# A fused attention and gated-MLP kernel: the first operand loaded in three pieces, five products over zeros ahead of the first scores, and a new table of due times

## The chip, the cores and the metric

The kernel runs on one core of one Trainium2 chip. The metric is device microseconds from launch to end; the kernel before was timed in three runs, with a median of 621.24 us (621.21 to 621.81). Differences of some tenths of a per cent are therefore about as small as can be told from no change.

Engines are named as the profile names them: PE is TensorE's matrix product, PEld its weight load, DVE is VectorE, ACT is ScalarE, POOL is GpSimd, and SP (SPq) is SyncE, which issues all of this kernel's transfers. Each engine works its own instructions strictly in the order in which the program lists them, so an instruction that waits holds back all that stand behind it on the same engine.

## The reference

```python
# q, k, v: (4, 12, 448, 64) f32; w_gate, w_val: (768, 1536); w_out: (1536, 768)
scores = np.matmul(q, k.T) / sqrt(64)             # causal: masked above the diagonal
attn = exp(scores - max);  attn = attn / (attn.sum(-1) + 1e-09)
x = np.matmul(attn, v)                            # reshaped to (1792, 768)
gate = 1.0 / (1.0 + np.exp(-(x @ w_gate)))
out = (gate * (x @ w_val)) @ w_out
```

## The kernel before, in words

There are 4 batches of 12 heads. Two heads make a pair (64 + 64 partitions), so there are 24 pairs, six to a batch. Per pair, `load` (L268) brings q and k, transposed, into a tile `raw` of 896 columns, and a small extra piece for the last block into a tile `sm`; `load_v` (L282) brings v. `score` (L288) computes the scores of the causal blocks 0 to 3, which have 128, 256, 384 and 448 keys, by `products` (L370, matmuls on L387). `softmax` (L398) takes each block from its PSUM tile with one masked minimum per head on DVE (L410), an exponential on ACT (L417), sums and a reciprocal on DVE (L426, L428) and a scaling on POOL (L438). In the opening, pairs 0 to 5, PE turns the result around (`trans`, L302, matmuls L313) and multiplies by v (`pv`, L326). From pair 6 on the turning is done by DVE and a trip through DRAM: `shift` (L442) writes a tile `tb`, sends it out (`pd<-tb`, L461) and brings it back in four pieces (`pt<-pd`, L464), and `wpv` (L468, matmuls L481) multiplies it by v (`vr`).

The MLP comes in two plain units (batches 0 and 1: `unit_items`, L582, matmuls L594) and one for batches 2 and 3 together (`pair_items`, matmuls L807). `weight` (L548) brings each weight block in as 64-bit words of 768 columns (`room<-in_wp`, L559), ACT and DVE turn it to f32 (L563, L565, L567), SP writes the f32 copy back (`wdram<-wr`, L570) for later units, and ACT with DVE or POOL splits it in a high and a low half (L575, L577). Every product of the MLP is three matmuls (high by high, high by low, low by high), each 448 columns wide; a group of six products, k = 0 to 5, fills one PSUM tile. The items of an attention step and of the MLP are merged on PE: as pairs of a batch are finished, the unit of that batch can start.

No order is written out by hand. `Plan.op` (L110) takes each step with its engine, a cost, what it reads and writes, and a due time. `Plan.order` (L156) hands due times back from each step to those it needs, adds a correction to some of them from the table `NUDGE` (L48, by the number of the step; L160), and then plays the program on a model of the engines: whenever an engine is free it takes, of the steps that the model has ready, the one with the earliest due time. The order of that play is the order in which each engine's instructions are emitted. A nudge below zero brings a step forward among those that are ready, one above zero puts it back; the chip then keeps to that order whatever is really ready.

`consts` (L248) builds the mask and the unit matrix on POOL. In `load`, pair 0 comes in two pieces, the first 512 and the last 384 columns; `_lay` (L1046) lays its columns out so that the first piece holds what blocks 0 and 1 need. Blocks 0 and 1 of a pair are one PE step, and their scores share one PSUM tile per head.

Of the kernel before, what the change touches and what calls it, by code (L numbers as in the profile page):

```python
# [8 lines left out]
F32 = mybir.dt.float32  # L9
# [198 lines left out]
def kernel(  # L208
# [21 lines left out]
    ident = new("ident", [128, 128], F32)  # L230
    mask = new("mask", [128, ZM + WQ + HALF], F32)
# [16 lines left out]
    def consts():  # L248
# [7 lines left out]

        fill(mask, 0.0)
# [10 lines left out]
    def load(n):  # L268
        j = pairs[n]
        j["raw"] = r = new("raw", [128, 2 * S], F32, BUFS["raw"])  # L270
        cols = (0, 4 * WQ, 2 * S) if n == 0 else (0, 2 * S)
        for e, (a, c) in enumerate(zip(cols, cols[1:])):
            keys_ = (e,) if n == 0 else (0, 1)
            plan.op("SP", dma(128 * (c - a) * 4), lambda a=a, c=c: nc.sync.dma_start(
                out=r.t[:, a:c], in_=qkt[n][:, a:c]), writes=[(r, *keys_)], extra=2.8)
# [12 lines left out]
    def score(n, blocks, due):  # L288
# [9 lines left out]
        needs = [(j["raw"], *((0,) if blocks[-1] == 1 else (0, 1)))] + ([(j["sm"][1], "x")] if blocks[-1] == 3 else [])  # L298
        burst((qk_cost(blocks), lambda: products(j, blocks), needs, [(p,) for p in sp]), due)
# [70 lines left out]
    def products(j, blocks):  # L370
        r, x = j["raw"], j["sm"][1]
        first = r is pairs[0]["raw"]
        q0 = lambda i: WQ * i + (S if first and i > 1 else 0)
        k0 = 2 * WQ if first else S
# [14 lines left out]
    def wscore(n, due):  # L389
# [5 lines left out]
        burst((1.95, lambda: products(j, range(NB)), [(j["raw"], 0, 1), (j["sm"][1], "x")], [(p,) for p in a + b]), due)  # L395
        return lambda: softmax(j, range(NB))

    def softmax(j, blocks):  # L398
        mn, su, r_ = j["mn"], j["sum"], j["r"]
        for i in blocks:  # L400
# [4 lines left out]
            for z in range(2):  # L405
# [7 lines left out]
                ), [(sp[z],), (mask, "end") if last and z else (mask,)] + ([(mn, (1, i))] if last and z else []),  # L413
                    [(sm, (i, z) if last else i), (mn, (to, i))])
            for z in heads:
                sm = j["sm"][z]
                plan.op("ACT", act(ne, 0, 1) + 0.01, lambda z=z, sm=sm, i=i, ne=ne, off=off: nc.scalar.activation(  # L417
# [677 lines left out]
```

## Time and profile before

| what | us |
|---|---|
| median of the runs (three) | 621.24 |
| the profiled execution, its own time | 620.8 |
| its span, first to last instruction | 619.1 |
| PE busy in it | 606.9 (98% of the span) |
| DVE, ACT, POOL busy | 439.7, 335.6, 310.6 |
| share of PE in the chain that ended last | 89% |
| PE's first and last product start | 3.47 and 615.07 |

The profile is one execution. A busy PE is one that has a product under way, so a product that waits before it starts is idle time, while one that runs at half pace is busy. The span is 1.7 us shorter than the time of the same execution, and that is 0.4 us below the median. The granted TensorE clock is 1.00 in all stretches. The DMA share is that of the core's 16 DMA engines.

### The profile page before, as it was taken

Reading aid. Unit: us, or ns where it says so; the run is one execution under the profiler, and the core shown is the slowest. Engines: PE = TensorE matmul, PEld = TensorE weight load, DVE = VectorE, ACT = ScalarE, POOL = GpSimd, SP = SyncE. Lnnn points to the kernel's source line nnn. Section 1 sums busy time; section 2 is a strip of 40 time slices with the busy share of each in tenths; the row PEclk is TensorE's granted clock in tenths of the full one; section 3 lists DMA queues with packets and bytes.
Section 4 is the critical chain, followed back from the end, with each engine's and each line's share of the span. In section 5 each row is a group of like instructions: output and inputs, shape, how many; then the busy total and the mean of one; then the engine's idle time right before and its main releaser. Section 6 shows DMA issues by size and latency. Waiting matters only on the chain.

```text
span 619.1 us, 11867 instructions
## 1 busy us (share of the span) xinstructions
PE 606.9 (98%) x4182; PEld 531.5 (86%) x4182; DVE 439.7 (71%) x1048; ACT 335.6 (54%) x754; POOL 310.6 (50%) x350
## 2 busy tenths in 40 slices
PE   6999999999999999999999999999999999999997
PEld 3578888898888888888888899989999989999996
DVE  5897999889855546544648766577754688999752
ACT  6996765675634755555558644434333443657420
POOL 5650534614300676767676676658664666611200
PEclk9999999999999999999999999999999999999999
DMA  8688999998999999878786886855533213534321
GB/s 299 203 308 314 344 370 378 376 397 320 364 396 339 321 365 344 293 245 319 269 323 247 281 311 238 276 199 189 179 110 95 77 52 103 159 117 142 112 75 60
DMA packets 54348, 153.35 MB, mean 248 GB/s; under 512 B 6032, under 2 KB 12432, under 8 KB 51984
## 3 DMA queue, kind: packets, MB, share of 16 engines
q1 hardware_dynamic: 54288, 152.59, 69.6%
q8 instruction: 33, 0.54, 0.3%
q14 instruction: 27, 0.22, 0.1%
HBM read 109.31 MB, written 43.25 MB: 246 GB/s over the span
## 4 chain that ended last, share of the span: by engine, by line
PE 89%; DMA 4%; DVE 3%; ACT 2%; issue 1%; POOL 0%; SPq 0%; DVEq 0%; ACTq 0%; POOLq 0%
PE m L594 39%; PE m L807 19%; PE s L807 10%; PE t L807 7%; PE m L481 5%; PE s L387 4%; PE t L387 2%; DMA raw<-in_qkt_dram 2%; DMA pd<-tb 1%; DMA vr<-in_vt_dram 1%; PE t L313 1%; ACT sm L417 1%; DVE wr L567 1%; DVE sm L410 1%; POOL sm L438 0%
## 5 line engine op out<-in xcount | busy, mean ns | idle before, releaser
L761 POOL TENSOR_TENSOR wl<-room,wh 128x384 fp32r<-128x384 f32 x84 | 98.0, 1190 | 56.0 <-ACT wh L760 56.0
L438 POOL TENSOR_SCALAR sm<-sm,r 128x384 f32<-128x384 f32 (+3 forms) x165 | 94.1, 591 | 63.6 <-DVE r L428 50.2
L594 PE MATMUL m<-xh,wh 128*128 128x448 f32 x288 | 107.3, 372 | 0.0
L594 PE MATMUL m<-xh,wl 128*128 128x448 f32 x288 | 105.3, 366 | 0.0
L594 PE MATMUL m<-xl,wh 128*128 128x448 f32 x288 | 105.2, 365 | 0.0
L417 ACT ACTIVATE sm<-sm,mn 128x384 f32<-128x384 f32 (+3 forms) x168 | 87.6, 524 | 18.6 <-DVE mn L410 15.2
L577 POOL TENSOR_TENSOR wl<-wr,wh 128x768 fp32r<-128x768 f32 x38 | 70.6, 1872 | 24.1 <-ACT wh L575 20.8
L575 ACT CAST wh<-wr 128x768 fp32r<-128x768 f32 x72 | 59.8, 832 | 33.4 <-DVE wr L567 15.0
L760 ACT CAST wh<-room 128x384 fp32r<-128x384 f32 x84 | 39.8, 511 | 52.5 <-PE s L807 12.7
L410 DVE CUSTOM_DVE_ANT_0 sm<-s,mask 128x128 f32<-128x128 f32 (+3 forms) x108 | 42.5, 408 | 25.8 <-PE s L387 25.7
L594 PEld LDWEIGHTS m<-xh,wh 128*128 128x128 f32 x288 | 54.1, 188 | 6.6 <-issue 1.6
L594 PEld LDWEIGHTS m<-xh,wl 128*128 128x128 f32 x288 | 54.1, 188 | 4.5
L594 PEld LDWEIGHTS m<-xl,wh 128*128 128x128 f32 x288 | 54.1, 188 | 4.1
L594 PE MATMUL m<-gh,wh 128*128 128x448 f32 x144 | 53.3, 370 | 0.0
L594 PE MATMUL m<-gh,wl 128*128 128x448 f32 x144 | 52.6, 365 | 0.0
L594 PE MATMUL m<-gl,wh 128*128 128x448 f32 x144 | 52.6, 365 | 0.0
L624 POOL TENSOR_TENSOR gl<-gt,gh 128x448 fp32r<-128x448 f32 x24 | 28.9, 1208 | 37.4 <-ACT gh L623 27.3
L807 PE MATMUL m<-pt,wh 128*128 128x448 f32 x150 | 44.8, 367 | 0.2 <-DVE xl L676 0.2
L453 DVE STREAM_TRANSPOSE room<-sm 128x384 f32<-128x384 f32 (+2 forms) x84 | 35.4, 449 | 8.8 <-POOL sm L438 8.4
L387 PE MATMUL s<-raw 64*64 64x128 f32 (+3 forms) x432 | 35.7, 390 | 4.6 <-DMA raw<-in_qkt_dram 3.5
L481 PEld LDWEIGHTS m<-pt,vr 128*64 128x64 f32 x720 | 33.5, 137 | 7.8 <-issue 4.3
L577 DVE TENSOR_TENSOR wl<-wr,wh 128x768 fp32r<-128x768 f32 x34 | 33.5, 984 | 7.9 <-ACT wh L575 7.4
(177 smaller groups left out, 1373.7 us busy)
## 6 DMA issues: line engine op xcount, KB each, us to landing
room<-in_wp_dram SPq DMA_DIRECT2D x36, 768.0 KB, 7.4
pt<-pd SPq DMA_DIRECT2D x72, 256.0 KB, 5.6
wr<-wdram SPq DMA_DIRECT2D x45, 384.0 KB, 4.6
room<-wdram SPq DMA_DIRECT2D x45, 384.0 KB, 3.6
wdram<-wr SPq DMA_DIRECT2D x36, 384.0 KB, 7.6
pd<-room SPq DMA_DIRECT2D x12, 1024.0 KB, 4.7
raw<-in_qkt_dram SPq DMA_DIRECT2D x23, 448.0 KB, 5.9
vr<-in_vt_dram SPq DMA_DIRECT2D x24, 256.0 KB, 5.3
```

What stands on the lines that cost most here:

```text
L387: nc.tensor.matmul(out=sp[z].t[c:c + 64, o:o + ne], lhsT=q, rhs=k)
L410: plan.op("DVE", dve(n), lambda z=z, i=i, sp=sp, sm=sm, n=n, o=o, f=f, lo=lo, to=to, first=first: nc.vector.tensor_tensor_reduce(out=sm.t[ ...
L417: plan.op("ACT", act(ne, 0, 1) + 0.01, lambda z=z, sm=sm, i=i, ne=ne, off=off: nc.scalar.activation(out=sm.t[:, off:off + ne], in_=sm.t[:, ...
L438: plan.op("PL", 0.24 + w / 1200, lambda sm=sm, e=e, o=o, w=w, z=z: nc.gpsimd.tensor_scalar(out=sm.t[:, o:o + w], in0=sm.t[:, o:o + w], sca ...
L453: plan.op("DVE", dve(128 * c) + 0.03, lambda sm=sm, i=i, o=o, c=c, at=at: nc.vector.transpose(out=tv()[:, :, at:at + 32 * c].rearrange("p ...
L481: nc.tensor.matmul(out=vp.t[64 * z:64 * z + 64, i * WQ:i * WQ + rows(i)], lhsT=v.t[:, c, z], rhs=src, start=(c == 0), stop=(c == i))
L575: plan.op("ACT", act(768), lambda: nc.scalar.copy(hi_.t, t.t), [(t,)], [(hi_,)])
L577: plan.op(eng, cost, lambda: at.tensor_tensor(out=lo_.t, in0=t.t, in1=hi_.t.bitcast(F32), op=ALU.subtract), [(t,), (hi_,)], [(lo_,)], lock ...
L594: nc.tensor.matmul(out=ps.t[:, :S], lhsT=a.t[:, k, :], rhs=b.t if isinstance(b, Buf) else b(), start=(first and z == 0), stop=(last and z ...
L760: plan.op("ACT", act(w), lambda: nc.scalar.copy(f(hi_.t), x()), [(src, at)], [(hi_, e)])
L761: plan.op("PL", 0.97, lambda: nc.gpsimd.tensor_tensor(out=f(lo_.t), in0=x(), in1=f(hi_.t).bitcast(F32), op=ALU.subtract), [(src, at), (hi_ ...
L807: nc.tensor.matmul(out=ps.t[:, :S], lhsT=a.t[:, kw, :], rhs=b.at, start=bool(first and z == 0), stop=bool(last and z == 2), skip_group_che ...
```

## The change

It has five parts.

1. `consts` gets a tile `idle` of 128 by 128, set to zero on DVE, and a PE step that multiplies it by itself five times into a PSUM tile that nobody reads. The step has due time 0.
2. `load` brings pair 0 in three pieces instead of two: 256 columns (what block 0 needs), 448 (the other keys, and block 1's queries) and 192 (the queries of blocks 2 and 3). `_lay` and `products` follow the new layout. A score step now waits for as many pieces as its block needs.
3. For pair 0, block 0 becomes a PE step of its own, due 0.3 ahead of block 1. In the planner DVE's read of a block now needs that block alone (the keys `(p, i)`), also in `wscore`.
4. The planner's cost of an exponential rises by 0.08.
5. The table `NUDGE` is replaced. Because four steps are new, a step with number n from 10 on has number n + 4 after. Among the entries that go: the first two weight loads (252 and 260, -9.6), and three steps of the trip through DRAM of one pair (808 and 811, +3.4, its DVE transposes; 813, +3.3, its `pd<-tb`). Among those that come: the load of pair 1's `raw` (43, -3.2); the load of one late pair's v (911, -6.1, was -0.9); the last DVE transpose and the `pd<-tb` of that pair (920 and 921, -2.6); and +9.8 to +12.4 on the product k = 1 of 16 weight groups (273, 337, 351, 367, 425, 441, 455, 471, 547, 561, 577, 743, 759, 803, 865, 879).

```diff
+    10: -6.1, 43: -3.2, 105: 5.3, 113: 2.4, 199: 2, 223: 14.4, 229: -6.4, 232: -5.5, 273: 9.8, 308: 3.8,
+    312: -1.1, 337: 9.8, 351: 9.8, 367: 9.8, 399: 4.9, 401: -0.5, 407: -6.5, 410: 4.9, 425: 9.8, 441: 9.8,
+    455: 9.8, 471: 9.8, 547: 9.8, 561: 9.8, 577: 9.8, 743: 9.8, 759: 9.8, 803: 9.8, 840: -1.8, 865: 12.4,
+    879: 12.4, 882: 2.6, 895: 2.6, 911: -6.1, 920: -2.6, 921: -2.6, 932: 1.8, 939: 4.8, 950: -1.7, 988: 3.4,
...
+    idle = new("idle", [128, 128], F32)
...
+        plan.op("DVE", 0.1, lambda: nc.vector.memset(idle.t, 0.0), writes=[(idle,)])
+        ps = new("t", [128, 512], F32, 2, PSUM)
+        plan.op("PE", 2.6, lambda: [nc.tensor.matmul(out=ps.t[:, :128], lhsT=idle.t, rhs=idle.t, start=True, stop=True)
+                                    for _ in range(5)], [(idle,)], [(ps,)], 0.0)
...
-        cols = (0, 4 * WQ, 2 * S) if n == 0 else (0, 2 * S)
+        cols = (0, 2 * WQ, S + 2 * WQ, 2 * S) if n == 0 else (0, 2 * S)
...
-        needs = [(j["raw"], *((0,) if blocks[-1] == 1 else (0, 1)))] + ([(j["sm"][1], "x")] if blocks[-1] == 3 else [])
-        burst((qk_cost(blocks), lambda: products(j, blocks), needs, [(p,) for p in sp]), due)
+        needs = lambda i: [(j["raw"], *range(min(i + 1, 3)))] + ([(j["sm"][1], "x")] if i == 3 else [])
+        if n < 1 and len(blocks) > 1:
+            for i in blocks[:-1]:
+                plan.op("PE", qk_cost((i,)), lambda i=i: products(j, (i,)), needs(i), [(p, i) for p in sp], due - 0.3)
+        here = blocks[-1:] if n < 1 else blocks
+        burst((qk_cost(here), lambda: products(j, here), needs(here[-1]), [(p, *here) for p in sp]), due)
...
-                ), [(sp[z],), (mask, "end") if last and z else (mask,)] + ([(mn, (1, i))] if last and z else []),
+                ), [(sp[z], i), (mask, "end") if last and z else (mask,)] + ([(mn, (1, i))] if last and z else []),
...
-                plan.op("ACT", act(ne, 0, 1) + 0.01, lambda z=z, sm=sm, i=i, ne=ne, off=off: nc.scalar.activation(
+                plan.op("ACT", act(ne, 0, 1) + 0.09, lambda z=z, sm=sm, i=i, ne=ne, off=off: nc.scalar.activation(
...
-    qkt[0] = np.concatenate([x[:, :2 * WQ], x[:, S:], x[:, 2 * WQ:S]], axis=1)
+    qkt[0] = np.concatenate([x[:, :WQ], x[:, S:], x[:, WQ:S]], axis=1)
```

## Rows read from the trace of the kernel before

**Rows 1.** Windows, by stage: length, busy PE, PEld, DVE, ACT, POOL, PEclk, DMA, GB/s.
```profile
3.47:10.00 6.53, 5.59 (x64) 3.12 (x64) 4.33 (x26) 4.47 (x17) 0.80 (x2) 1.00 0.94 292
20.00:40.00 20.00, 18.94 (x231) 11.70 (x222) 17.84 (x74) 17.77 (x56) 14.95 (x23) 1.00 0.77 255
80.00:120.00 40.00, 40.00 (x304) 35.37 (x304) 36.58 (x89) 25.41 (x55) 18.41 (x25) 1.00 1.00 376
160.00:182.00 22.00, 20.21 (x160) 18.28 (x159) 14.18 (x25) 8.77 (x13) 3.13 (x7) 1.00 1.03 397
```
**Rows 2.** Timeline of PE, 3 to 8 us: start, length, operation, count, idle before.
```profile
3.47 1.56 PE L387 MATMUL s<-raw 64*64 64x128 f32 x16 [3.47 <-DMA raw<-in_qkt_dram]
4.80 1.50 PE L387 MATMUL m<-raw 64*64 64x384 f32 x8
...
7.31 0.88 PE L387 MATMUL m<-raw 64*64 64x384 f32 x8 [0.46 <-DMA raw<-in_qkt_dram]
```
**Rows 3.** Timeline of PE around 28 us: the same first step of a later pair.
```profile
27.72 0.88 PE L387 MATMUL s<-raw 64*64 64x128 f32 x16
```
**Rows 4.** The chain that ended last, 40 to 60 us: start, length, what.
```profile
44.37 0.87 PE t L313 x8
```
**Rows 5.** Memset of a tile as large as the new one, on POOL, by tile.
```profile
L250 POOL MEMSET ident<- x1: 204/204/204, 1.3 to 1.3; 128x128 f32 x1
```
**Rows 6.** Timeline of SP's queue in the opening.
```profile
0.80 0.86 SPq L274 DMA_DIRECT2D raw<-in_qkt_dram  x2
...
2.18 0.43 SPq L274 DMA_DIRECT2D raw<-in_qkt_dram  x1
...
6.87 3.74 SPq L274 DMA_DIRECT2D raw<-in_qkt_dram  x2
```
**Rows 7.** Window of the first transfers, columns as in the first group.
```profile
1.75:3.42 1.67, 0.00 (x0) 0.00 (x0) 0.00 (x0) 0.33 (x1) 1.32 (x6) 1.00 0.92 288
```
**Rows 8.** Issue to landing, by tile: the first two pieces of pair 0.
```profile
DMA to landing us min/median/max: 2.6/2.6/2.6
```
**Rows 9.** Issue to landing: the small extra piece issued at 1.72 (`sm`).
```profile
DMA to landing us min/median/max: 4.2/4.2/4.2
```
**Rows 10.** Issue to landing: pair 1's load, issued at 2.18 (`raw`).
```profile
DMA to landing us min/median/max: 5.1/5.1/5.1
```
**Rows 11.** Timeline of DVE in the opening.
```profile
5.20 0.29 DVE L410 CUSTOM_DVE_ANT_0 sm<-s,mask 128x128 f32<-128x128 f32 x1 [5.20 <-PE s L387]
...
5.62 0.42 DVE L410 CUSTOM_DVE_ANT_0 sm<-s,mask 128x256 f32<-128x256 f32 x1
...
8.93 0.25 DVE L410 CUSTOM_DVE_ANT_0 sm<-s,mask 128x128 f32<-128x128 f32 x1
```
**Rows 12.** Timeline of PE, 160.9 to 162.7 and 178.9 to 180 us.
```profile
162.59 0.33 PE L481 MATMUL m<-pt,vr 128*64 128x128 f32 x2 [1.23 <-DMA vr<-in_vt_dram]
...
179.94 0.33 PE L481 MATMUL m<-pt,vr 128*64 128x128 f32 x2 [0.56 <-DMA vr<-in_vt_dram]
```
**Rows 13.** Timeline of SP's queue, 144 to 174 us.
```profile
144.42 0.33 SPq L559 DMA_DIRECT2D room<-in_wp_dram  x1
144.80 0.43 SPq L570 DMA_DIRECT2D wdram<-wr  x1
145.34 0.36 SPq L461 DMA_DIRECT2D pd<-tb  x1
...
153.05 2.55 SPq L464 DMA_DIRECT2D pt<-pd  x4
155.64 0.47 SPq L285 DMA_DIRECT2D vr<-in_vt_dram  x1
...
173.41 0.44 SPq L285 DMA_DIRECT2D vr<-in_vt_dram  x1
```
**Rows 14.** Issue to landing: the last two `pt<-pd` pieces issued near 172 us.
```profile
DMA to landing us min/median/max: 7.0/7.1/7.2
```
**Rows 15.** Timeline of PE, 20 to 22 us.
```profile
21.06 0.87 PE L387 MATMUL s<-raw 64*64 64x128 f32 x14 [0.62 <-DVE mn L410]
```

More of the change, by code (lines that the diff above doesn't have):

```diff
@@ L270, in load @@
         j["raw"] = r = new("raw", [128, 2 * S], F32, BUFS["raw"])
-        cols = (0, 4 * WQ, 2 * S) if n == 0 else (0, 2 * S)
+        cols = (0, 2 * WQ, S + 2 * WQ, 2 * S) if n == 0 else (0, 2 * S)
         for e, (a, c) in enumerate(zip(cols, cols[1:])):
-            keys_ = (e,) if n == 0 else (0, 1)
+            keys_ = (e,) if n == 0 else (0, 1, 2)
             plan.op("SP", dma(128 * (c - a) * 4), lambda a=a, c=c: nc.sync.dma_start(
@@ L372, in products @@
         first = r is pairs[0]["raw"]
-        q0 = lambda i: WQ * i + (S if first and i > 1 else 0)
-        k0 = 2 * WQ if first else S
+        q0 = lambda i: WQ * i + (S if first and i else 0)
+        k0 = WQ if first else S
         for i in blocks:
@@ L394, in wscore @@
         j["sp"] = {0: (a, 384), 1: (b, 0), 2: (a, 0), 3: (b, 256)}
-        burst((1.95, lambda: products(j, range(NB)), [(j["raw"], 0, 1), (j["sm"][1], "x")], [(p,) for p in a + b]), due)
+        burst((1.95, lambda: products(j, range(NB)), [(j["raw"], 0, 1, 2), (j["sm"][1], "x")], [(p, 0, 2) for p in a] + [(p, 1, 3) for p in b]), due)
         return lambda: softmax(j, range(NB))
```

12 rows, old and new, of the table NUDGE are left out of this document.

## The prediction

> **What bounds the kernel now.** I read the windows by stage first, then the chain that ended last, then the timelines of PE, DVE and SP in the two places where PE stands. In the windows the reader is to see that PE is busy for all 40 us of a middle stretch, and that the idle time of PE lies in three places: ahead of its first product at 3.47 and in the opening behind it (5.59 busy of 6.53, and 18.94 of 20.00 later), and 1.79 us in the 22 us from 160 on [rows 1, 2]. Whatever starts the full stretch earlier, or fills those 1.79 us, moves the end by as much; the products themselves are the same before and after. The second thing to see is that in the first third PE is not far ahead of its helpers: DVE is at 36.58 of 40 us and the DMA engines at a share of 1.00 there [rows 1]. So the end of that stage hangs on PE and on the transfers at once, and a lead that PE gains in the opening can be waited off at 160.
>
> **Working against which time.** The sum is made on the profiled execution: span 619.1, its own time 620.8, so 1.7 around it. The median of the runs, 621.24, is 0.4 above that; I take the sum off the median.
>
> **The opening.** Now: PE starts when the first piece has landed, at 3.47, and its 16 first products take 1.56 us, where the same step of a later pair takes 0.88; the next eight take 1.50 against 0.88 for the same shape at 7.31 [rows 2, 3]. These are half-pace against full-pace durations (1.2 and 2.4 GHz), though the granted clock is told as 1.00 throughout: what PE did before was nothing at all. Together they cost 0.68 + 0.62 = 1.30 us. DVE, which must take every block out of PSUM, starts at 5.20 because blocks 0 and 1 are one step [rows 11].
>
> The dummy products: a memset of this size took 0.20 us on POOL [rows 5]; DVE is free from 0.8 on (SP's first issue is at 0.80 [rows 6]), so PE can begin at about 1.1. Eight 128-column f32 records took 0.87 us at full pace [rows 4]; five products are ten records, 1.1 us at full pace and 2.2 at half. I take 2.2, since nothing ran before: they end at about 3.3 (bounds 2.2 and 3.3 by the row; by the planner's own cost of 2.6, at 3.7). The first piece has half the bytes: 131 KB less at 288 GB/s is 0.46 us off a landing at 0.80 + 2.6 = 3.4, so about 2.95 [rows 6 to 8]. The data no longer decide, the dummies do: block 0 starts at 3.3 instead of 3.47, at half pace takes 0.5 (a third of 1.56), and with the 0.17 from the last product to DVE's first read [rows 2, 11] DVE starts at about 4.0: 1.2 us earlier. The second piece, 229 KB, ends 98 KB later than the first piece of before, 0.34 us, so at 3.8, in time for block 1.
>
> What is late next: pair 1's load lands at 2.18 + 5.1 = 7.3, and PE waited 0.46 us for it [rows 2, 6, 10]. The third piece costs SP one more issue, 0.43 us (0.86 for two [rows 6]); but step 43 at -3.2 puts pair 1's load ahead of pair 0's small extra piece (by the planner's rule for due times the two stood at 2.8 and 0.3), so it is again the fourth issue, at 2.18. Step 10 at -6.1 is the second piece; the planner lets no write go before the first one of a tile, so nothing moves. It can land up to 0.5 us earlier (147 KB, 0.5 us at 288 GB/s [rows 7]), and the small piece, now landing at 1.72 + 4.2 = 5.9 [rows 9], falls to about 7.3. So DVE will have done blocks 0 to 2 of pair 0 by about 6.2 and then stand for about 1 us. It had all of pair 0 behind it at 8.93 [rows 11]; then it will have block 3 left, about 1.3 us with its sums, at 7.3, and be there at 8.3 to 8.6. **The lead that gets through is 0.3 to 0.6; bounds 0 (pair 1's load decides alone) and 1.2 (the whole of DVE's start). I take 0.6.**
>
> The first two weight loads lose their -9.6 and fall behind the loads of later pairs, among them the one issued at 6.87 [rows 6]. The bytes are the same, and the products that need them come late in the opening, whose transposes PE still works on at 44.37 [rows 4]; I cost this at nothing, covered by the opening's attention work of some 20 us, and at up to 1 us if that cover went. The 0.08 in the cost of an exponential and the keys in the planner change no instruction.
>
> **The stage at 160 to 182.** PE stands 1.23 us before the product at 162.59 and 0.56 us at 179.94, both times until v has landed; that is the whole 1.79 of the window [rows 1, 12]. First stand: `pd<-tb` is issued at 145.34, right behind a weight load (786 KB) and a write-back (393 KB) at 144.42 and 144.80; its return starts at 153.05 and v is issued behind it at 155.64 [rows 13]. The +3.3 that held this `pd<-tb` back, and the +3.4 on its transposes, are gone, so it should go ahead of those 1.18 MB, which at 397 GB/s are 3.0 us of transfer [rows 1]. The last transposes end just before 145.34, so the issue itself moves little; the landing can move by up to 3.0. That more than covers 1.23. Behind SP's wait for the transposes then stand the weight load and the write-back, delayed about 1 us; their readers are ACT and DVE in the queue for a later group. Second stand: v's load is brought forward by 5.2 more than before, ahead of the four return pieces; then the last return piece, which landed at about 172.0 + 7.2 = 179.2 [rows 14], is late next, 0.7 before 179.94: worth about 0.5. **Together 1.7 at most. I take 1.4; bounds are 0 (the wait only moves to the next transfer) and 1.79.**
>
> **The held products.** Sixteen products k = 1 are due 9.8 to 12.4 later, which is about twelve products of 0.6 us, so attention steps between them may go up to 7 us earlier on PE. PE has no idle time there to win, 40.00 of 40.00 [rows 1]. The gain is that scores reach DVE sooner, the cost that PE may stand at a step whose data are not there. Nothing in the trace shows the new order; bounds: -1.06, the idle time of 20 to 40 us [rows 1] filled, and +1.23 for one stand like that at 162.59 [rows 12]. I take 0, midway, because both rows are near.
>
> **Sum:** -0.6 - 1.4 + 0 = -2.0 us, span 617.1, median **619.2**.
>
> **A rule that speaks against the split.** The nearest row for a product that waits for a DVE read of scores is at 21.06: 0.62 us [rows 15]. Blocks 0 and 1 share one PSUM tile per head, so when DVE reads block 0 as block 1 is to be written, block 1 may have to wait until both heads are read: 5.20 to 5.62 and a short tail, about 0.5 us [rows 11]. Then DVE stands while block 1 runs, and blocks 0 to 2 end 0.5 to 0.7 later, at 6.9, still ahead of 7.3: the lead drops by 0.3, to a median of 619.5. The Trainium skill's page "PSUM — Partial Sum Buffer", section "PSUM bank collisions raise a hardware error", says that two engines must not be in one bank and partition quadrant at the same time, whatever columns they touch, and that software has to guard it; by that rule block 1 would wait. No row of the kernel before shows a write beside a read in one tile, so this is open.
>
> **The rivals.**
> *Bank wait*, as just priced: 619.5.
> *Absorbed.* The transfers, at a share of 1.00, keep their times, and PE only arrives earlier and waits longer. For it: DMA at 1.00 and 1.03 in the two stretches [rows 1], and both stands end with a transfer. Against it: the DMA share is 0.77 at 20 to 40 us, so the transfers too can start earlier. It gives 621.24 less nothing to 0.4: 621.0.
> *Warm-up does nothing.* PE runs the dummies at half pace, stands, and the scores still come at half pace or later (3.7 by the planner's cost): the lead is -0.2 to 0, the rest stays: about 620.0, just on the line.
> *Slower: the held products.* An attention step reaches PE before its last transfer or its DVE read is done, and PE, in order, stands there with ready MLP products behind it. There are six such steps, those of pairs 6 to 11. It decides against the change when two of them stand 1.3 us each beside the two stands that stay, which grow by the lead: +2.6 - 0.6 = +2.0, 623.2. For it: the planner's due times run ahead of the chip (the load issued at 155.64 stood in it under a due time of 143.6), so what its model has ready need not be ready. Against it: the same planner, equally off, gives 40.00 of 40.00 before.
>
> **How the numbers follow.** Forecast (619.2) 0.37, bank wait (619.5) 0.13, warm-up nothing (620.0) 0.10, half on each side, absorbed (621.0) 0.25, slower (623.2) 0.15. A measurement of this kernel tells 0.2%, 1.2 us, from no change: faster means below 620.0, slower above 622.5. Faster 0.55, same 0.30, slower 0.15. The range leaves out the slower rival and the far end of the gains: from 621.24 - 1.2 - 1.79 - 0.9 = 617.4 (both places at their bounds and most of the 1.06) to 621.9 (absorbed, with half a stand of 1.23 more).
>
> **What would show it.** Opening: PE's first product at about 1.1, block 0 at about 3.3, the 64x384 products at nearer 0.88 than 1.50, DVE's first read near 4.0; if pair 1's products still start at 7.3 the lead is what the steps say. Bank wait: block 1 starts only as DVE's second read ends. Stage: idle time of PE between 150 and 185 well below 1.79, `pd<-tb` ahead of the weight load, v not the last releaser. Held products: PE idle in the windows from 40 to 160 us, now 0. I am wrong if the wait for v only moves to the return pieces, or if PE's idle time appears at new attention steps.

## The result: slower by 0.9%, and the profile after

The changed kernel takes **627.6 us** (median of four runs, 627.01 to 628.37) against 621.52 for the kernel before: a ratio of 1.0089, with an interval of 1.0068 to 1.0111. The prediction was 619.2, range 617.4 to 621.9. The span of the profiled execution is 626.3 against 619.1: 7.2 us to account for.

To find where they lie I summed the columns of all matmul records in order of time (weighted by what a column of their shape takes at full pace, the products over zeros left out) and read how much later the changed kernel reaches each sum. This **lag** behind the profiled execution of the kernel before is used for all kernels below.

| time in the kernel before, us | 5 | 10 | 20 | 30 | 50 | 160 | 165 | 170 | 180 | 220 | 230 | 360 | 390 | 615 |
|---|---|---|---|---|---|---|---|---|---|---|---|---|---|---|
| lag of the changed kernel, us | 0.91 | 1.65 | 0.71 | -0.18 | 1.32 | 1.32 | -0.14 | 1.30 | 0.72 | 0.65 | 5.86 | 5.88 | 7.09 | 7.06 |

So 5.2 of the 7.1 us come at one place, between 220 and 230, and 1.2 more at 380. The opening and the stage at 160 to 182, on which the whole sum of the prediction stood, come out at a loss of 0.7 together: 1.3 lost by 50 us, and 0.6 won back between 160 and 180. From 50 to 160, where the held products lie, nothing changes.

**The opening.** Timeline of TensorE in the changed kernel (start, length, operation, count, idle before and its releaser); it answers to [rows 2]. Lines of the changed file lie 11 higher from the products on.

```profile
1.12 2.50 PE L262 MATMUL t<-idle 128*128 128x128 f32 x10 [1.12 <-DVE idle L260]
3.55 0.71 PE L398 MATMUL s<-raw 64*64 64x128 f32 x8
4.78 1.33 PE L398 MATMUL s<-raw 64*64 64x256 f32 x8 [0.52 <-DVE mn L421]
5.69 1.71 PE L398 MATMUL m<-raw 64*64 64x384 f32 x8
...
7.71 1.89 PE L398 MATMUL m<-raw 64*64 64x384 f32 x8
```

The five products run from 1.12 at half pace and end at 3.62, and block 0 follows at 3.55, no earlier than in [rows 2]; what comes sooner is its end, 4.26, since block 1 is no longer part of the step. Then TensorE waits 0.52 us, and not for data: the releaser is VectorE, which has to have read block 0 from the tile that block 1 goes into. The 64x384 products take 1.71 and 1.89, where [rows 2] has 1.50 and then 0.88: half pace lasts longer. VectorE, to be read against [rows 11]:

```profile
4.42 0.29 DVE L421 CUSTOM_DVE_ANT_0 sm<-s,mask 128x128 f32<-128x128 f32 x1 [3.36 <-PE s L398]
...
6.15 0.42 DVE L421 CUSTOM_DVE_ANT_0 sm<-s,mask 128x256 f32<-128x256 f32 x1 [1.22 <-PE s L398]
...
10.54 0.29 DVE L421 CUSTOM_DVE_ANT_0 sm<-s,mask 128x128 f32<-128x128 f32 x1 [0.78 <-PE s L398]
```

It reads block 0 at 4.42 instead of 5.20, block 1 at 6.15 instead of 5.62, and is at pair 1 at 10.54 instead of 8.93. The trace's record of the granted clock starts with the first stretch at full: at 9.97 us here, at 6.37 in the kernel before. Ahead of it the views print 1.00 for want of a record, which is why the windows show no change there; the durations do. So "1.00 in all stretches", as it stands ahead of the prediction, does not hold for the first 6.37 us of the kernel before.

**The two large places.** Windows of the changed kernel (columns as in [rows 1]), then its timeline of TensorE:

```profile
80.00:120.00 40.00, 39.85 (x302) 34.91 (x301) 36.90 (x91) 27.42 (x59) 16.03 (x21) 1.00 0.99 363
160.00:182.00 22.00, 20.94 (x150) 18.59 (x150) 15.52 (x22) 9.42 (x14) 2.33 (x4) 1.00 1.01 379
224.00:234.00 10.00, 6.24 (x72) 5.30 (x64) 3.09 (x17) 2.31 (x8) 3.34 (x4) 0.83 0.96 337
```

```profile
169.97 0.48 PE L605 MATMUL m<-gh,wl 128*128 128x448 f32 x1 [1.06 <-DVE wl L588]
...
229.04 3.34 PE L492 MATMUL m<-pt,vr 128*64 128x128 f32 x40 [3.76 <-DMA pt<-pd]
232.31 0.47 PE L605 MATMUL m<-xh,wh 128*128 128x448 f32 x1
...
381.08 2.00 PE L492 MATMUL m<-pt,vr 128*64 128x128 f32 x40 [0.91 <-ACT wh L771]
```

In the first window TensorE is busy for 39.85 of 40 us: the held products bring no stand. In the second it is 20.94 busy where [rows 1] has 20.21: the stands for v at 162.59 and 179.94 [rows 12] are gone as predicted, but one of 1.06 for a weight split has come at 168.9. At 225 TensorE stands 3.76 us for the probabilities of a pair to come back from DRAM (`pt<-pd`); the granted clock falls to half in that stand (0.83 over the window), and the 40 matmuls behind it take 3.34 us, where the same group of a later pair, at 381, takes 2.00. 3.76 + 1.34 = 5.1, the step of the table. SyncE's queue and GpSimd say why the return is late; SyncE in the changed kernel, then in the kernel before, then GpSimd in the changed kernel:

```profile
212.36 0.38 SPq L472 DMA_DIRECT2D pd<-room  x1
213.53 2.14 SPq L583 DMA_DIRECT2D wr<-wdram  x2
215.72 0.65 SPq L745 DMA_DIRECT2D wd<-wdram  x1
220.08 0.32 SPq L472 DMA_DIRECT2D pd<-room  x1
220.50 3.88 SPq L475 DMA_DIRECT2D pt<-pd  x4
```

```profile
210.06 0.33 SPq L461 DMA_DIRECT2D pd<-room  x1
...
215.90 1.80 SPq L464 DMA_DIRECT2D pt<-pd  x4
217.80 0.38 SPq L274 DMA_DIRECT2D raw<-in_qkt_dram  x1
220.97 0.32 SPq L461 DMA_DIRECT2D pd<-room  x1
```

```profile
206.50 2.67 POOL L449 TENSOR_SCALAR sm<-sm,r 128x384 f32<-128x384 f32 x5 [0.71 <-DVE r L439]
209.14 1.84 POOL L588 TENSOR_TENSOR wl<-wr,wh 128x768 fp32r<-128x768 f32 x1
210.95 0.73 POOL L449 TENSOR_SCALAR sm<-sm,r 128x128 f32<-128x128 f32 x2
```

A pair's probabilities go out at 212.36 and have landed at 219.26, but its four returns stand behind the *next* pair's send, which waits for VectorE's transposes until 220.08. So they go out from 220.50 and the last lands at 228.84; in the kernel before they went out from 215.90 to 217.27, ahead of that send, and had landed at 222.68, 1.7 us before TensorE came to them at 224.42.

So the last landing is 6.2 us later, for two reasons. The send itself is late: two of the pair's seven scalings now stand behind a weight split on GpSimd, so the send leaves 2.30 us later (212.36 for 210.06) and takes 6.90 us to land instead of 5.33, together 3.9. The rest, 2.3, is the order on SyncE: the returns start 1.24 us behind that landing instead of 0.51, and take 8.34 us from the first issue to the last landing instead of 6.78. The two don't simply add up in the stand. An estimate from these numbers: with the late send but the returns ahead of the next send, the last would land at 219.26 + 0.51 + 6.78 = 226.55, and TensorE, which is there at 225.28, would stand 1.3 us instead of 3.76. With the send in time but the returns behind the next send, they would still go out at 220.50, and the stand would be the same. So by this estimate the order carries most of the stand; no run changes it here without the send.

### The profile page after: what moved, and what is told of

Read it like the earlier page. It is cut to its first block, busy times and chain, and to the rows that moved or that the text cites. A ratio compares the mean times of both kernels' runs of the same rounds, so it can differ in the third digit from the quotient of the medians.

```text
span 626.3 us, 11881 instructions
## 1 busy us (share of the span) xinstructions
PE 613.2 (98%) x4192; PEld 536.6 (86%) x4192; DVE 446.1 (71%) x1049; ACT 334.9 (53%) x754; POOL 310.7 (50%) x350
## 4 chain that ended last, share of the span: by engine, by line
PE 84%; DVE 5%; DMA 5%; ACT 2%; POOL 1%; issue 1%; SPq 1%; DVEq 0%; ACTq 0%; POOLq 0%
PE m L605 35%; PE m L818 19%; PE s L818 10%; PE t L818 7%; PE m L492 5%; PE s L398 3%; DMA room<-in_wp_dram 3%; DMA pt<-pd 2%; PE t L398 2%; DVE sm L421 1%; POOL sm L449 1%; PE t L324 1%; DVE wl L588 1%; SPq L475 1%; DVE wr L578 1%
## 5 line engine op out<-in xcount | busy, mean ns | idle before, releaser
L449 POOL TENSOR_SCALAR sm<-sm,r 128x384 f32<-128x384 f32 (+3 forms) x165 | 91.8, 577 | 79.1 <-DVE r L439 57.5
L772 POOL TENSOR_TENSOR wl<-room,wh 128x384 fp32r<-128x384 f32 x84 | 96.4, 1168 | 60.4 <-ACT wh L771 56.4
L428 ACT ACTIVATE sm<-sm,mn 128x128 f32<-128x128 f32 (+3 forms) x168 | 87.7, 525 | 15.7 <-DVE mn L421 15.3
L492 PEld LDWEIGHTS m<-pt,vr 128*64 128x64 f32 x720 | 34.9, 141 | 10.8 <-issue 8.6
L492 PE MATMUL m<-pt,vr 128*64 128x128 f32 (+1 forms) x720 | 37.3, 260 | 4.8 <-DMA pt<-pd 3.8
L574 ACT ACTIVATE wd<-room 128x768 f32<-128x768 f32 x36 | 32.6, 911 | 17.1 <-DMA room<-in_wp_dram 17.1
```

The source lines that it names most:

```text
L428: plan.op("ACT", act(ne, 0, 1) + 0.09, lambda z=z, sm=sm, i=i, ne=ne, off=off: nc.scalar.activation(out=sm.t[:, off:off + ne], in_=sm.t[:, ...
L449: plan.op("PL", 0.24 + w / 1200, lambda sm=sm, e=e, o=o, w=w, z=z: nc.gpsimd.tensor_scalar(out=sm.t[:, o:o + w], in0=sm.t[:, o:o + w], sca ...
L492: nc.tensor.matmul(out=vp.t[64 * z:64 * z + 64, i * WQ:i * WQ + rows(i)], lhsT=v.t[:, c, z], rhs=src, start=(c == 0), stop=(c == i))
L574: plan.op("ACT", act(n) + 0.1, lambda: nc.scalar.activation(out=d.t.bitcast(F32), in_=hi().bitcast(F32), func=ACTF.Prelu, scale=REBIAS, al ...
L772: plan.op("PL", 0.97, lambda: nc.gpsimd.tensor_tensor(out=f(lo_.t), in0=x(), in1=f(hi_.t).bitcast(F32), op=ALU.subtract), [(src, at), (hi_ ...
```

## The experiments

All times are medians, and each ratio is to the kernel before, run beside it on the same chip; it need not be the quotient of two medians. Runs of one kernel spread over 1.6 to 6.3 us there (the kernel before: 620.3 to 626.7 in 141 runs), so ratios below 1.002 are hardly told from 1. Part of this spread has a name: in 32 of the 141 runs the mean granted clock is 0.997 or less, and they take 623.3 us at the median, the others 621.3. A profile is one execution and can be of either kind: those of f3, g3, h2 and h6 have a stretch at half clock, and for f3, g3 and h2 they lie 1 to 3 us above the median of their kernel. "Without N" and "with N" speak of entries of the table `NUDGE`, by the numbers of the changed kernel unless it is said otherwise (its steps are numbered four higher from the opening on).

**1. Which part costs the 6 us?** Four runs on the changed kernel and the one before.

```diff
 e1 (changed kernel)  -    1074: 2.9, 1075: 2.9, 1076: 2.9, 1077: 2.9,
 e2 (changed kernel)  its code; NUDGE = the table before, numbers + 4
 e3 (kernel before)   its code; NUDGE = the new table, numbers - 4
 e4 (changed kernel)  -  lambda: [nc.tensor.matmul(...) for _ in range(5)]   +  lambda: None
```

> The changed kernel without the four entries 1074 to 1077 (+2.9), which put the POOL scalings of one pair back. PE's order stays the same; in SP's queue the four return pieces of that pair come ahead of the next pair's send again. Theory A (the loss is one stand of PE at 225 us, set off by these entries): the stand of 3.8 us and the half-pace product group behind it (3.3 instead of 2.0) go, about -5 us, 622.4. Rival B (the loss is the opening, and the stand only shows a lead being waited off): the wait moves to a later product, 627 or more.

> The changed kernel's code (three pieces, five products, block 0 a step of its own) with the due-time table of the kernel before, every number plus 4. It tells the price of the code alone. Theory A: the code costs what the opening loses, 0.6 to 1.6 us, so 622.1 to 623.1, and there is no stand at 225. Rival B (the code carries most of the loss): 626 or more. My prediction's steps would have given 620.9.

> The kernel before with the new due-time table alone, every number minus 4 (entry 10 left out). Theory A: the stand at 225 us and its half-pace group come all the same, about +5 and +1 for the wait at 380: 626.5 to 627.5. Rival B: 621.5.

> The changed kernel with the five products over zeros not issued; order of everything else the same, so the output is unchanged. Theory: in the opening PE goes over to full pace at 9.97 us instead of 6.37 because block 1 waits for DVE, not because of the products; without them block 0 starts at 3.1 instead of 3.55 and the rest of the opening is within 0.5 us of the changed kernel, 627.1 to 627.6. Rival 1 (the products do warm PE): full pace comes later still, pair 1 takes longer, 628 to 629. Rival 2 (the products themselves put the change of pace off): full pace near 6.4, opening 1 to 1.5 us shorter, 626.3.

| run | us | ratio (interval) |
|---|---|---|
| e1 without four scalings' entries | 622.38 | 1.0009 (0.9991 to 1.0026) |
| e2 new code, old due times | 622.72 | 1.0026 (1.0011 to 1.0041) |
| e3 old code, new due times | 630.69 | 1.0145 (1.0120 to 1.0171) |
| e4 changed, no products | 627.12 | 1.0082 (1.0059 to 1.0106) |

Most of the cost lies in the table: e2 and e3 part code from table (the code alone costs 0.1 to 0.4%), and e1 shows that without four of its entries the stand at 225 is gone (lag 0.14 at 220, 0.24 at 230; the end 1.4). Those four are what puts the two scalings behind the weight split: the last one ends at 211.68 in the changed kernel and at 209.35 in e1, where the send leaves at 209.96 and the returns at 216.43, ahead of the next send. e3 came out 3 us above its expectation: with the old code the new table stands at 228.8 too (2.33), and besides loses 4.5 us between 15 and 40 us, whose cause I did not follow up. Leaving the products out (e4; nothing reads what they compute) changes nothing that can be measured.

**2. Is it those four entries, or the order that they make on SyncE?**

```diff
 g4 (kernel before)  +    1070: 2.9, 1071: 2.9, 1072: 2.9, 1073: 2.9,
 h1 (kernel before)  +    917: -2.6, 1073: 2.9, 1106: 6.8, 1123: 8.2, 1157: 0.6,
 h4 (kernel before)  +    917: -2.6,            1106: 6.8, 1123: 8.2, 1157: 0.6,
```

> The kernel before with 2.9 us added to the due times of four of its steps (1070 to 1073, the scalings that 1074 to 1077 are in the changed kernel; 1072 loses its own 0.5) and nothing else; the order of TensorE is unchanged, on GpSimd two of seven scalings fall behind a weight split, and on SP the four transfers that bring the probabilities back (pt<-pd) fall behind the next pair's room load. Theory A (these four entries alone are the cost): a stand of 2 to 4 us for pt<-pd between 220 and 230, with the 40 matmuls behind it at half pace if it is long: 625 to 627. Rival B (they cost only together with the rest of the new table): no stand there, 621.5.

> The kernel before with five entries of the new table (917, 1073, 1106, 1123 and 1157 here; 921, 1077, 1110, 1127 and 1161 in the changed kernel) added to its own: the smallest set found by which the planner again puts the four transfers that bring a pair's probabilities back (pt<-pd) behind the next pair's send (pd<-room) on SP. On TensorE one step changes place by three. Theory A (that order on SP is the cost of the changed kernel): a stand of 2.5 to 4 us for pt<-pd at 225, followed by 40 matmuls at half pace where the clock falls: 624 to 627. Rival B (the order alone costs little; it takes the late transposes or the rest of the table as well): 621.5 to 622.5.

> The same without the entry 1073, that is with four of the five: TensorE's order is the one of the run with five, but SP issues the four pt<-pd before the next pair's send, as in the kernel before. Theory A: no stand at 225, 621.5 to 622.2. Rival (the other four entries are the cost): 624 or more, as with five.

g4: 622.19 (1.0006, 0.9989 to 1.0024), no stand at 225. Its send is 1.3 us late too (211.40), but against its expectation the returns stay ahead of the next send (216.30 and 220.75). So the four entries do nothing alone; my theory fell in that form. In the planner's play the return falls behind the next send only when several small moves add up: played with one entry of the changed kernel's table left out at a time, it has the old order again for any one of 932, 988, 1074, 1077, 1087 and 1110. h1 is the smallest such set that I found for the kernel before, h4 the same without one of its five; both have the same order on TensorE. **h1: 628.40 (1.0105, 1.0081 to 1.0128), somewhat above its expectation. h4: 621.85 (1.0010, 0.9996 to 1.0025).** SyncE's queue and TensorE's timeline, h1 first, then h4:

```profile
212.94 0.38 SPq L455 DMA_DIRECT2D pd<-room  x1
...
220.94 0.32 SPq L455 DMA_DIRECT2D pd<-room  x1
221.36 3.37 SPq L458 DMA_DIRECT2D pt<-pd  x4
```

```profile
229.17 3.68 PE L475 MATMUL m<-pt,vr 128*64 128x128 f32 x40 [3.56 <-DMA pt<-pd]
232.78 0.74 PE L588 MATMUL m<-xh,wh 128*128 128x448 f32 x1
```

```profile
209.98 0.33 SPq L455 DMA_DIRECT2D pd<-room  x1
...
215.69 1.80 SPq L458 DMA_DIRECT2D pt<-pd  x4
219.82 0.32 SPq L455 DMA_DIRECT2D pd<-room  x1
```

```profile
224.34 2.00 PE L475 MATMUL m<-pt,vr 128*64 128x128 f32 x40
```

In h1 the returns are behind the next send, TensorE stands 3.56 us and goes on at half pace (3.68; 0.74 for the product behind it, where 0.37 is usual); in h4 they are ahead of it and the same group starts without a wait at 224.34. The lag of h1 goes from 0.97 at 220 to 7.11 at 230, that of h4 is about 0 at both. One due time tells the two kernels apart, and nothing else of the change is needed for the whole loss. That due time does two things, as in the changed kernel: it puts a scaling behind a weight split on GpSimd, so that the send leaves 3.0 us later (212.94 for 209.98), and it turns the order on SyncE. By the same estimate as above the late send alone would leave 1.7 of the 3.56 us.

**3. What does the opening give?** Block 0 gets tiles of its own (f1, f2, f4, g1), with and without the products; the products alone (g3); ones in place of zeros (g1).

```diff
 f1 (e1)             +        if n < 1 and len(blocks) > 1:
                     +            j["sp"][0] = ([new("t", [128, 512], F32, 2, PSUM) for z in range(2)], 0)
 f2 (f1)             as e4
 g3 (kernel before)  + the memset of `idle` and the five products, as in the change
 f4 (e2)             f1's edit; without 812, 815, 817; 911: -6.1
 g1 (f4)             - memset(idle.t, 0.0)   + memset(idle.t, 1.0)
```

> The changed kernel without entries 1074 to 1077 (as in the run with four scalings undone, 622.4), and block 0 of the first pair gets two PSUM tiles of its own, so that block 1's products need not wait until VectorE has read block 0. Theory A (the 0.5 us pause between block 0 and block 1 is what keeps TensorE at half pace until 9.4): products and scores run without a break from 1.1 us, the full clock is granted by 6.4 us at the latest, VectorE reads block 1 at about 5.2 instead of 6.16, TensorE stands ahead of the kernel before at 10 us by some 0.5 instead of 1.46 behind. Rival B (something else keeps the pace down): the full clock still comes after 8.5 us and the first reads of pair 1 at 10.3 or later. On the time: if an early lead is carried on, 621.4; if it is used up before 30 us, as the lag of 1.46 at 10 us was there, 622.4 as without the edit.

> The same without the five products over zeros (the step issues nothing; they compute nothing that is used). Theory A (an unbroken run of TensorE work brings the full clock): scores start at 2.9, the full clock comes about 2.9 us later, as in the kernel before (3.47 and 6.37), so near 5.9, some 1 to 2 us later than with the products; the time is within 0.4 us of the run with products. Rival (products are what brings the full clock): without them it comes after 8.5 us, as in the run without products and with shared tiles (9.4).

> The kernel before with the five products over zeros and their memset ahead of the first scores and nothing else of the change (its own due times; a handful of steps behind 250 us change places because the play starts otherwise). Theory A (the products don't bring the full clock forward, it follows the scores): full clock 2.9 to 4.5 us after the first scores, between 6.4 and 8, as in the three profiled runs of this code so far (6.37, 7.65, 7.92), time 621.5. Rival B (the change's aim): the scores that start at 3.5 run at full pace from 5 us at the latest, the first reads of pair 1 come 0.4 us or more earlier than 8.93, time 621.0.

> The kernel with own tiles and old due times (621.4, full clock from 6.65), with ones in place of zeros in the tile that the five products read. Rival A (products over zeros don't count as work for the clock): with ones the full clock comes before 5.5. Rival B (what the numbers are makes no difference): between 6.4 and 8. The time is the same, 621.4, in both, since an earlier clock meets the landing of pair 1's raw at 8.1.

| run | full clock from, us | first read of pair 1, us | lag at 10 us | us | ratio (interval) |
|---|---|---|---|---|---|
| before | 6.37 | 8.93 | 0 | | |
| g3 before, products | 7.18 | 9.11 | 0.12 | 621.71 | 1.0010 (0.9989 to 1.0030) |
| e1 shared tile, products | 9.39 | 10.36 | 1.46 | 622.38 | 1.0009 (0.9991 to 1.0026) |
| f1 own tiles, products | 7.52 | 9.50 | 0.88 | 622.05 | 1.0006 (0.9991 to 1.0021) |
| f2 own tiles, no products | 9.02 | 10.11 | 1.21 | 623.13 | 1.0008 (0.9988 to 1.0029) |
| f4 own tiles, old order | 6.65 | 9.71 | 0.75 | 621.37 | 0.9990 (0.9975 to 1.0005) |
| g1 the same, ones | 4.70 | 9.72 | 0.77 | 622.34 | 1.0006 (0.9993 to 1.0020) |

Own tiles take the pause away: TensorE in f1, and then in g1.

```profile
3.55 0.83 PE L392 MATMUL t<-raw 64*64 64x128 f32 x8
4.03 1.20 PE L392 MATMUL s<-raw 64*64 64x256 f32 x8
4.89 1.62 PE L392 MATMUL m<-raw 64*64 64x384 f32 x8
```

```profile
4.81 0.86 PE L392 MATMUL m<-raw 64*64 64x384 f32 x8
5.46 0.69 PE L392 MATMUL s<-raw 64*64 64x224 f32 x4
5.96 0.60 PE L392 MATMUL s<-sm 64*64 64x224 f32 x4
8.15 0.88 PE L392 MATMUL m<-raw 64*64 64x384 f32 x8 [1.59 <-DMA raw<-in_qkt_dram]
```

Three things follow. The bank wait is real and goes with the shared tile. When the full clock comes varies from execution to execution: the old opening without products, seven profiled executions of as many kernels, has it from 6.37 to 9.23; unbroken with products, eight, 4.70 to 7.52 (the early ones at 5.33 and 5.37 are with zeros, so ones are not what makes the 4.70); with products and the pause, three, 8.58 to 9.97; pause and no products, two, 9.02 and 9.41. So the products bring it forward by 0.8 us at the median (7.65 to 6.82), and the pause goes with the late end (f2, with tiles of its own, pauses too, 0.50 us until the second piece has landed); but the groups overlap, and one execution of each kernel doesn't settle more. And little of it gets through: in g1 the last two blocks of pair 0 ran at full pace, and then TensorE stands 1.59 us until pair 1's operand has landed at 8.10. That is the old order of the loads, in f4 and g1. With the new one pair 1's operand lands earlier, at 6.46 to 7.12, and TensorE waits for pair 0's own small piece instead, which lands at 7.20 to 7.46 in g2, h5 and f1; in g2:

```profile
7.24 0.41 PE L392 MATMUL s<-sm 64*64 64x224 f32 x2 [0.88 <-DMA sm<-in_qkt_dram]
```

In no run does the new opening reach pair 1's first read before 9.16 us, however early its clock, against 8.93 to 9.29 in five of the seven with the old one. My expectation that f1 would be ahead at 10 us was wrong. That the products are worth nothing is not shown with tiles of their own: f2, without them, takes 623.13 where f1 takes 622.05, and the intervals of their ratios overlap.

**4. Where does the gain at 160 go, and can both be had?**

```diff
 f3 (kernel before)  without 808, 811, 813; 907: -6.1            (its own numbers)
 h6 (kernel before)  new entries for 796 to 995 in place of its own
 g2 (f1)             the old table from step 1300 on
 h2 (f1)             the old table from step 300 on
 h3 (h2)             and the new one from 800 to 999
 h5 (h3)             +    plan.behind(plan.ops[2251], plan.ops[1944])
                          order = plan.order()
```

> The kernel before with four entries of its own table changed and nothing else: 808, 811 and 813 are left out, and 907 (the load of vr that TensorE waits for at 162.59) gets -6.1 instead of -0.9, as its counterpart has in the changed kernel. If the two stands of the kernel before at 161 and 179 (1.23 and 0.56 us) are worth what the prediction took for them, 1.4 us, the time is 620.1 against 621.5, with neither stand in the trace; if what follows uses the gain up, or another stand takes its place, 621.5.

> The kernel before with the new due times for its steps between 796 and 996 in place of its own there, and nothing else of the change. Theory A (the stand at 161 goes by these entries alone, as the prediction had it): no stand at 161, 0.6 to 1.4 below the kernel before: 619.7 to 620.5. Rival (it takes the lead that the opening gives as well): the stand stays, 621.1 or more.

> The code of the changed kernel with block 0 in PSUM tiles of its own and the old due times (shifted by the four new steps) with the same four entries changed. The run with the old due times in the changed code gave 622.7, with a stand of 1.03 at 162.6 and 0.6 of lag from 25 us on. Theory A: the stand at 162.6 goes (-1.0 to -1.2) and the opening loses its 0.5 us pause and the late full clock (-0.5 to -1): 620.5 to 621.2, level with the kernel before or a little ahead. Rival: the opening's gain is used up within the first 40 us and the stand moves: 622 to 622.7.

> The kernel with own tiles and new due times without 1074 to 1077 (622.05; profiled: level with the kernel before at 360 us, 1.7 behind from 380 on, after a stand of 1.43 at 374), with the old due times from step 1300 on. Theory A (the entries behind 1300 are what puts the load before the stand at 374 late): no stand there, the end 1.4 to 1.7 earlier: 620.5. Rival B (the stand follows from the earlier part or from the code): it stays, 622.

> Own tiles for block 0, the products and three pieces, the new due times for steps below 300 and the old ones from there on. In the two profiled runs with own tiles and the new table TensorE stood 0.9 and 1.2 us ahead of the kernel before at 30 us and lost it between 30 and 50 and in the stands behind. Theory A (what was lost came of the new entries behind 300): the lead is carried to the end: 620.5. Rival B (the lead is used up by 50 us whatever the table says): 621.5 to 622.

> The same with the new due times between 800 and 1000 too, where the stand at 161 (1.23 in the kernel before) goes. Theory A: 0.6 to 1.2 below the run with steps below 300 alone. Rival B (the stand of 0.8 to 1.1 for the weight split at 168 takes its place, as in the four runs without the stand at 161): within 0.4 of it.

> The run with new due times below 300 and between 800 and 1000 (620.56), with one more order on SP and on no other engine: the prefetch of a weight for the last stage (step 2251, wr<-wdram, due at 504), which waited at 365.4 for its buffer with a pair's four pt<-pd behind it, is put behind them. Theory A (a transfer that stands on SP holds all behind it, as at 225): the four go out when their send has landed, 363.7, some 1.7 earlier; the stand of 0.74 at 372 goes and the 1.07 lost between 360 and 390 stays: 619.5 to 619.9. Rival (it moves to the next limit): 620.3 to 620.6.

| run | stands of TensorE from 160 us on | us | ratio (interval) |
|---|---|---|---|
| f3 | 161.6: 2.68 | 621.66 | 0.9995 (0.9978 to 1.0012) |
| h6 | 178.2: 1.89 | 622.07 | 1.0003 (0.9987 to 1.0019) |
| f4 | 168.7: 0.79 | 621.37 | 0.9990 (0.9975 to 1.0005) |
| g2 | 168.7: 1.05 | 621.81 | 0.9999 (0.9986 to 1.0011) |
| h2 | 161.6: 1.90; 226.4: 0.48 | 622.06 | 1.0005 (0.9986 to 1.0024) |
| h3 | 372.1: 0.74 | **620.56** | 0.9983 (0.9968 to 0.9998) |
| h5 | 178.9: 0.70 | **620.19** | 0.9966 (0.9952 to 0.9981) |

Four entries don't close the stand at 161 in the kernel before (f3: the send still leaves behind a weight load, at 146.83, and v lands at 164.17, 1.7 later than before). The length of that stand varies by itself, though: 1.23, 1.18 and 2.93 us in the profiles of the kernel before, g4 and g3, which have the same due times there. The entry 907 is that of the v waited for at 179.94, not at 162.59 as the expectation says, and the stand at 179 is gone in f3. The whole middle of the table closes the stand at 161, but alone (h6) the next limit takes over, 1.89 at 178.2 with the clock at half behind it. In the changed kernel, e1, f1 and g2, and in f4 and g1 with the old table but for the four entries, a weight split is late at 168 to 170 instead, and most of the lag gained by 165 is lost again. With the new middle and the old entries behind it (h6, h3, h5) there is no such stand, and h3 keeps the gain: its lag goes from -0.48 at 160 to -2.27 at 180. h5, with the same table, gains 1.2 there. h2, the same without the middle, has the old stand at 161 again. f4 lies just behind the near end of its theory. h2 went to its rival, and so did g2 in its time, though the stand at 374 is gone there: the lead of 0.6 to 1.3 at 30 us, which all runs with own tiles and the new opening have, is spent by 50 us whatever the later entries are; on what, I did not follow up.

The medians hide one more thing. In the 80 runs of e1, f1, f2, f4, g1, g2 and h5, whose profiles have no stand at 161, the mean granted clock is never below 0.999; in those of the kernel before it is at 0.997 or less in 32 of 141, and in f3, g3 and h2 the half clock comes in that stand or just behind it.

h3 loses 1.1 between 360 and 390 at a stand that e1 and f1 also have (0.77 and 1.43), and the changed kernel one of 0.91 at 380; h5 changes nothing but SyncE's order there. SyncE in h3, then in h5:

```profile
359.61 0.32 SPq L466 DMA_DIRECT2D pd<-room  x1
361.05 2.51 SPq L577 DMA_DIRECT2D wr<-wdram  x2
365.43 0.32 SPq L739 DMA_DIRECT2D wr<-wdram  x1
365.84 2.05 SPq L469 DMA_DIRECT2D pt<-pd  x4
```

```profile
359.51 0.32 SPq L466 DMA_DIRECT2D pd<-room  x1
360.97 2.49 SPq L577 DMA_DIRECT2D wr<-wdram  x2
364.57 1.74 SPq L469 DMA_DIRECT2D pt<-pd  x4
```

In h3 the returns wait behind the prefetch of a weight that nobody needs before the last stage, and that itself waits for its buffer until 365.43; the last lands at 372.62, and TensorE, there since 372.12, stands. The kernel before has this order too (its last return lands at 373.03) and no stand, since its TensorE comes 1.9 us later: the lead is what meets the limit. With the prefetch put behind them, the returns go out at 364.57, as soon as their send has landed (364.51), and the last lands at 371.22, 1.4 earlier. That is what an order on SyncE does with no other engine's order changed. TensorE has no stand at 372 in h5, but that it is the order that ends it is not shown: this execution is 1.6 us behind h3's by then and comes to the group at 373.65, when h3's returns had landed too. h5 beats the kernel before by 0.34% (interval 0.19 to 0.48), so a table with the gain at 160 and without the loss at 225 can be had; it fell 0.3 short of its expectation, and its lead over h3 is within the intervals of the two.

## Why the prediction was wrong, point by point

- **The step that failed** is the one that gave the table nothing. The sum has a term for the opening, one for 160 to 182, and one for sixteen held products (0, between -1.06 and +1.23). The entries for steps 1069 to 1161, scalings, a send and its returns, have no term at all, and they carry +5.2 of the 7.1 us. I priced steps one by one, by the engine that issues them, and didn't ask what several small moves do together to one transfer: the scalings come late on GpSimd and the send with them, and on SyncE, where everything behind a waiting transfer waits too, its returns fall behind the next send. The profile of before had the numbers: the last of these returns landed at 222.68, 1.7 us before it was needed, and the next send stood waiting until 220.97. There was 1.7 us to lose, and the table lost 6.2.
- **The slower rival** had the mechanism (TensorE, in order, before a transfer that hasn't landed, with ready MLP products behind), but not its place, nor its cause, and with 1.3 per stand not its size: one stand of 3.76, and 1.34 on top for a group at half pace, which no term foresaw.
- **The opening** was sized at -0.6 and cost 1.3, outside its bounds: the lag is 1.65 at 10 us, and, after a dip at 30, 1.32 at 50 and still at 160. The transfers came as the sum has them: the first two pieces landed at 2.89 and 3.84 (2.95 and 3.8 in the sum), pair 1's load at 6.74 (6.8 to 7.3), the small piece at 7.11 (7.3). TensorE's pace did not. The products over zeros took 2.50 us, not 2.2. The bank wait, a rival at 0.13, came: 0.52 us against the 0.5 worked out there. The Trainium skill's page "PSUM — Partial Sum Buffer", section "PSUM bank collisions raise a hardware error", asks for such a guard by bank and not by address; the trace agrees, block 1 waits for the read of block 0 in other columns. And half pace lasted until 9.97, where the sum went by a profile with the full clock from 6.37, the earliest of the seven with the old opening; that the one profile of before was this one was chance. "Warm-up does nothing" was right in effect for the change (e4, g3): in the changed kernel the full clock comes no earlier than without the products (9.97 and 9.41). Where own tiles take the pause away it does come earlier, and then the transfers, at the share of 0.94 that [rows 1] shows for the opening, decide when TensorE can go on. That is the *absorbed* rival's mechanism, which I had at 0.25.
- **160 to 182** was sized at -1.4 and gave 0.6. Both stands went as the step says: in the changed kernel the send leaves at 143.83, ahead of the weight load, and lands 3.4 us earlier (149.57 for 152.95; the sum has up to 3.0), and at the second place the last return lands at 179.27 (179.2). But it is not the entries named that do it, as f3 shows, and the weight split at 168 gave 1.06 back. In h3 and h5, with other due times behind it, the same place gives 1.8 and 1.2, the far bound and a little less than the size taken. The mechanism was right; what moved the send was put down to too few entries, and "what is late next" was asked for v alone.
- **The held products** came out at the 0 that was taken, the middle between two bounds: the lag is 1.32 at 50 and at 160.
- **The range** reached to 621.9 on the side of the loss, since it left out the slower rival, and even that one, at 623.2, held no single stand above 1.3.

## What to carry to other kernels

When steps are reordered, write down for each in-order queue, SyncE's first, which transfer will stand at its head waiting and what lies behind it: here a send 2.3 us late and its return behind another item's send cost 5 us, and 6.5 between h1 and h4, where the order on TensorE is the same. Note beside it how long each landing comes before it is needed; 1.7 us was all there was. Price a reordering by pairs of steps that change places, not step by step. Before speeding up an opening, look which transfers the rest of the first item and the second one start on; what is won ahead of them is waited off there.

## What the runs showed of the hardware that was not expected

- A stand costs more than its length when the clock falls in it or just behind it. After stands of 3.76 (changed kernel), 3.56 (h1), 3.43 (e4), 2.93 (g3), 2.68 (f3), 1.90 (h2) and 1.89 (h6) the granted clock was at half, and the group of 40 matmuls behind took 3.34, 3.68, 3.68, 3.52, 3.07, 3.23 and 3.15 us instead of 2.00; after 2.33 (e3), 1.81 (h1), 1.64 (h4) and 1.03 (e2) it took 2.00. The length of the stand alone does not tell. The Trainium skill's page "TensorE: Matmul & The Clock Gate", section "HAM oscillation — how this bites in real kernels", describes such a fall behind a wait for a transfer; the trace agrees.
- The start of the full clock differs between executions by up to 2.9 us for the same first products (6.37 to 9.23 in seven executions with the old opening). One profile of an opening says little about a warm-up.
